# Half swaps strided by two into buffers that are tiles of their own, split input tiles and a new order, in a one-core block of long convolution and MLP

## The chip, the core and the metric

The kernel runs on one core of a Trainium2 chip. The metric is the device time of the program in microseconds (us). The kernel before takes 302.73 us, the median of three runs (301.24, 302.73 and 303.07).

The engines are named as in the profile: PE (TensorE, matmul; PEld its weight loads), DVE (VectorE), ACT (ScalarE), POOL (GpSimd) and SP (SyncE, which here only issues DMAs). L613 is line 613 of the kernel before.

## What is computed

All tensors are bf16, with S = 2048 tokens, D = 640 channels and F = 1728. The reference, cut to what matters:

```python
mod = (silu(c) @ w_mod).reshape(6, D)          # sa, ca, ga, sb, cb, gb
h = layernorm(x) * (1 + ca) + sa               # x is A_q
x = x + ga * A(h, k, v, shift_k, ssm_k, ssm_D)
h = layernorm(x) * (1 + cb) + sb
x = x + gb * B(h, w1, w2, w3, w4)

def A(q, k, v, ...):
    kv = shift_conv(k, 4 taps) * v
    y = irfft(rfft(kv, 4096) * rfft(ssm_k, 4096))[:2048]   # along the tokens, by channel
    return q * (y + kv * ssm_D)

def B(h, ...):
    g = gelu(layernorm(h) @ w1)                # its four quarters are shifted by 1, -1, 2, -2 tokens
    h1 = h + shifted(g) @ w2
    return h1 + gelu(layernorm(h1) @ w3) @ w4
```

## The kernel before

**Order.** The body does not issue instructions directly. It makes tasks (`add`, L90), each with the engines that may run it, and the ranges that it reads and writes. A string `ORDER` (L26 to L66) lists all 1046 tasks by number, each with a letter for its engine (P for PE, D for DVE, A for ACT, G for POOL, S for SP) and, for PE, the PSUM slots (four, 0 to 3) that it takes. `run` (L120) emits the tasks in that order. Each engine works through its own tasks in the order of the list and waits where an operand is not there yet. The order of a DMA queue is thus also an order of the list.

**Memory.** The large buffers are single tiles that are used several times over: Ra (ssm_k, then x), Rb (slots, tables of products, then y), T01 with its halves T0 and T1, R3 (first the spectrum of ssm_k), R5 (k and v, then the spectrum of kv), RG (stage-2 tables), RH, RK and RQ.

**FFT stage.** ssm_k is loaded (L228) and k and v are loaded transposed (L233), in five blocks of 128 channels. L444 folds ssm_D into the first element of ssm_k. `k_shift` makes the shift convolution with diagonal weights on PE (L463) and multiplies by v on DVE (L468). `to_slots` (L394) transposes 32x32 blocks on DVE. The Fourier transform of length 4096 has two steps of matmuls: `stage1` (L407) against F1bd, and `stage2_half` (L427) against tables Gs in RG. The tables hold sines and cosines that are made here: angles (L287 to L294, or L302 to L310 with POOL), Sin on ACT (L316, L321), a negated copy (L348), and copies over the partitions by DMA (L353, L354). In the output of stage 2, the real parts are in partitions 0 to 63 and the imaginary ones in 64 to 127. Results leave PSUM by ACT (L207) or DVE (L209).

**inverse1** multiplies the two spectra, ten blocks of 128x2048. A product of complex numbers needs one factor with its real and imaginary halves exchanged. Two DMAs of 256 KB (L613) make that copy of the block `kx` into one of four buffers KSY (a part of RG, two of RK, one of Rb); the first is issued by SP and the second by POOL. DVE then makes two products (L617), PE multiplies them by EA and EB (L628, L629; made at L370), and ACT or DVE evicts.

```python
for o in range(2):
    dma("SP" if o == 0 else "POOL", 256, lambda q, o=o: q.dma_start(
        ky[64 * o:64 * o + 64, :], kx[64 - 64 * o:128 - 64 * o, :]), ...)
```

**inverse2** (L661) needs all of inverse1 and tables in RH (L576 copies them there by 16 DMAs), takes groups of up to three token tiles and two PSUM slots at a time, and its result y goes to Rb.

**Transition and MLP.** x is loaded by `x_load` (L525), tiles 0 to 7 early, 8 to 11 and 12 to 15 later. Statistics of the first layer norm come by L539 and L540 on DVE, or L547 and L548 on ACT. The modulation vectors are products on PE (L493), evicted at L508. `make_q` (L592, L594, L601, L602) normalizes and modulates a tile, `chain_a` (L737, L740) multiplies by y and adds to x, `square_sum` (L729, ACT) and `ln_finish` (L702 to L717, with a power on POOL at L715) give the statistics, `chain_b` (L755, L756) the second modulation, and `chain_c` (L594 or L724) normalizes and turns the tile over by PE (L772; copied at L778 or L780) or by a DMA transpose (L765). Then `mm_w1` (L818, L828; gelu at L820, L834), `mm_w2` (L873; L880 on DVE), `mm_w3` (L907; gelu at L911) and `mm_w4` (L928, L937; L960 to L966 on DVE), and the output is stored (L969, and L987 for the last tile). w1 and w2 are loaded at L992 to L995 into RG, w3 at L1012 into T0, w4 into T1. The buffers g3 of the second gelu are in R5.

Of the kernel before, what the change touches and what calls it, by code (L numbers as in the profile page):

```python
# [8 lines left out]
BF = mybir.dt.bfloat16  # L9
# [17 lines left out]
0S 2S 19G 18D 50G 20D 21G 23D 22D 25A 4S 3S 1S 6S 27G 29D 36G 37G 28D 5S 8S 9S 11S 68G 10S 69D 24A 26G 88P:0 72G 73D 31A 30A 32D 38G 66D 89A 84P:1 85A  # L27
67D 90P:2 91A 86P:3 87D 39G 40A 102P:0 103A 100P:1 76P:2 70G 104P:0 41D 49G 101A 77A 42G 43G 105A 106P:3 107A 44A 45G 33S 47S 46S 71D 34S 12S 35S 48S
184S 181S 183S 182S 13S 14S 116P:1 92P:2 98P:0 74D 75D 117D 7S 99A 118P:3 119D 114P:0 15S 112P:1 113D 93A 110P:2 16S 115A 111A 96P:3 97A 94P:0 95D
82P:2 83A 80P:1 81A 78P:3 108P:0 51D 109A 52D 54A 56G 57D 53A 122P:2 79D 155P:1 156A 153P:0 154A 151P:3 152A 123D 157P:2 136D 120P:1 121D 173P:0 158A  # L30
55G 174A 171P:3 172A 177P:2 178D 175P:1 176A 161P:0 162D 141P:3 142A 167P:2 168D 147P:1 148A 58G 59G 163P:0 164D 165P:3 166A 137P:2 138A 145P:1 146A
230D 17S 149P:0 150A 190D 188D 126P:3 127D 139P:2 140A 60A 143P:1 199S 144A 124P:0 125D 179P:2 180A 187D 169P:3 170A 234P:1 235A 244P:2 159P:0 160A
128P:3 231D 242P:1 243A 245A 130P:0 61G 62G 186D 63G 64A 238P:1 239A 129D 131D 232D 248P:2 65G 196S 249A 246P:3 247A 185D 189G 191A 252P:0 202S 253A
134P:1 135D 132P:2 133D 236P:3 240P:1 237A 260P:0 261A 233D 250P:2 251A 241D 423D 200P:3 201A 258P:0 259D 319G 208S 192G 268P:2 269A 318S 197P:3 205S
198A 266P:1 267A 272P:2 273D 270P:3 271A 203P:0 284P:1 285A 292P:2 211S 204D 278P:3 279A 417D 276P:0 277A 342S 293D 426D 209P:1 210D 294P:2 295D 226S
290P:3 222G 291A 280P:1 281D 229G 227S 264P:0 274P:2 275D 343G 223G 265A 256P:3 262P:1 420D 206P:0 207D 257A 225G 254P:2 255D 282P:3 263A 286P:0
288P:1 287D 224G 312P:2 220S 283A 289A 212P:3 321D 320D 218G 213D 313A 328D 304P:0 305A 308P:1 316P:2 317A 217S 216G 302P:0 219S 214G 418D 228S 298P:2
215S 324P:3 325D 309A 221G 327G 326S 329D 322P:1 303A 336D 306P:0 299A 421D 323A 310P:2 296P:3 307A 334S 335G 337D 350S 297A 311A 300P:1 330P:0 301A
351G 332P:3 344D 345D 331A 314P:2 333A 315A 359G 340P:1 341A 338P:0 352D 348P:3 349A 353D 346P:2 358S 347A 360D 361D 354P:1 367G 339A 356P:3 368D 366S
369D 355A 364P:2 357A 375G 362P:0 376D 372P:1 374S 377D 401S 193A 363A 382S 370P:3 373A 384D 383G 385D 380P:0 378P:1 365A 392D 390S 391G 393D 422D  # L40
419D 424D 402P:2 427D 194D 403D 371A 388P:3 381A 379A 407S 389A 428D 386P:0 387A 416G 425D 396P:1 397A 394P:3 395A 398S 399P:0 400D 432P:12 429A 430D
434D 433A 489D 502A 510D 195G 413S 490D 491A 511D 530D 408P:3 513D 404S 405P:0 406A 531D 409A 512A 440S 492G 494D 475P:12 476A 477A 515D 532A 462P:03
463A 410S 411P:1 493G 495D 514G 435S 533D 534G 496A 497D 498G 441G 535D 464A 516D 536D 518D 499D 412A 517A 469P:20 537A 471A 519G 500P:3 538D 539G
414P:1 465G 470A 558D 449S 501D 520D 521P:3 436S 415A 507P:0 522A 443S 559D 560A 540D 541P:2 437S 542A 466P:13 431D 561D 562D 563A 564D 508A 546P:2
467D 468A 547A 548P:1 565G 448S 570D 528P:0 571D 566D 572D 567D 549A 573A 446S 568D 505P:3 506A 569A 574G 575G 447S 509G 529A 503D 523D 504D 621D 622D
472P:21 473A 526P:3 527A 623A 579D 580P:0 581A 576D 439S 543A 524D 577P:2 525D 624D 578D 625D 444S 438S 550P:3 627D 480S 551D 481S 626A 590P:0 591A
445S 482S 552A 588P:2 589A 595P:3 459D 628G 633D 629D 634D 553G 630D 631D 632A 635D 637D 636A 479S 554G 555D 556P:0 557A 592P:2 486S 596D 597A 638G
641A 639D 478S 488G 610P:3 612P:0 611A 593D 608P:2 606P:3 544D 594A 598D 613A 599G 474D 460A 603D 600D 601P:1 604P:0 609A 457D 607A 442S 454A 602A
640S 642S 651P:2 649P:3 461G 650A 450D 487S 652A 485S 605D 673P:0 667P:1 451D 545D 668A 674A 452G 582D 583D 484S 689D 690D 456A 458G 584D 585D 656P:3
692D 693D 653P:2 483S 614P:1 654D 655A 657D 694A 615D 659G 658A 671P:0 695D 660G 664D 665P:2 691A 661D 662P:3 663D 453D 669P:1 696G 701A 702D 703D  # L50
666A 735P:3 455G 672A 670A 697D 698D 699D 705G 737P:2 736A 739P:0 733P:1 616D 704A 643D 644D 645D 700A 738A 706G 709A 675P:32 710S 586D 587D 740A 755D
756D 757A 646A 707D 708S 758D 759D 717P:0 714D 761G 760A 762G 734A 763A 767D 777A 768D 711A 769D 719P:1 764D 780D 676P 718A 720A 721P:0 724P:1 647D
712D 765D 766A 677D 678D 770A 680S 771G 772G 683D 741P:32 648D 773D 774S 722D 775A 776S 785P:0 725D 726A 783P:1 713D 723A 824D 617S 825D 742P 821D
822D 827D 679S 681S 826A 743D 682S 727G 728G 731D 732S 823A 784A 828G 829A 786A 787P:3 729D 730S 833D 834D 835D 830D 831D 832A 837D 684D 685S 836A
620S 838G 790P:1 788D 789A 839D 840S 799P:0 791D 805P:3 806A 781D 841D 715D 716D 881D 749D 793G 792A 882D 842S 883A 803P:1 804A 794G 795A 796S 845P:2
846A 797D 778D 779D 884D 843P:3 844A 885D 887D 800A 801P:1 802A 618S 847P:2 848D 782D 941D 850P:3 851D 852A 886A 849A 619S 687S 798S 865P:0 866A
859P:1 860A 863P:2 807P:30 861P:1 744D 750D 753S 942D 944D 745S 853D 854G 855A 888G 893A 943A 752S 857A 889D 864A 945G 890D 856S 808P 858S 809D 891D
946A 947D 948D 950D 894D 862A 892A 895D 896A 897G 925P:2 926A 898G 751S 815D 747S 919P:3 901D 686S 920A 923P:1 899D 921P:0 949A 951G 922A 902S 900S
905P:2 906A 688S 903P:3 904A 952D 953S 956P:0 957A 954P:2 955A 907P:3 908D 910P:0 810D 958G 748S 959P:2 911D 913G 746S 816D 819S 924A 962P:1 867P:30
960D 817S 963D 813S 754S 912A 993P:2 909A 914G 812S 868P 915D 916S 917D 918S 977P:1 978A 994D 995A 996G 997G 971P:2 820S 972A 869D 998A 875D 927P:30  # L60
818S 964A 814S 811S 876D 961A 965D 966G 973P:1 967A 999S 969A 970S 870D 929D 974A 1028P:2 930D 975P:3 928P 968S 1000P:1 1001A 931S 935D 1002P:0 934S
976A 979P:13 981D 1003A 1006P:0 871S 873S 1004P:1 879S 1005A 872S 874S 936D 980P 987D 1029A 937S 933S 1026P:1 939S 1007A 877S 932S 988D 1024P:2 1025A
1032D 880S 878S 982D 983S 1008P:30 986S 991S 1027A 989S 1033D 1010D 938S 940S 1022P:2 1011D 1023A 1014S 1013S 1009P 1016D 984S 985S 1017D 1030P:13
1034D 992S 990S 1015S 1012S 1018S 1019S 1020S 1035D 1037S 1036S 1021S 1038S 1031P 1040D 1039S 1041D 1043A 1045A 1042S 1044S
# [72 lines left out]
def kernel(  # L137
# [20 lines left out]
    Ra = mem.tile([P, 10240], BF, name="Ra")  # L158
# [6 lines left out]
    RK = mem.tile([P, 4096], BF, name="RK")  # L165
# [9 lines left out]
    sT = Ra[:].rearrange("p (b n) -> p b n", b=ND)  # L175
    sL = Rb
    kvL = Rb
    x_all = Ra[:].rearrange("p (a d) -> p a d", d=D)
# [4 lines left out]
    Gs = RG[:, 0:6144].rearrange("p (k n) -> p k n", k=32)  # L183
# [6 lines left out]
    wm = [(R[:, o:o + 1600].rearrange("p (b n) -> p b n", b=ND), (k, o, o + 1600)) for R, k, o in ((RH, "RH", 0), (RH, "RH", 1600), (RK, "RK", 0))]  # L190
    TAB = [[Rb[:, (2 * i + j) * 2048:(2 * i + j + 1) * 2048] for j in range(2)] for i in range(2)]
    KSY = [(RG[:, 6144:8192], ("RG", 6144, 8192)), (RK[:, 0:2048], ("RK", 0, 2048)), (RK[:, 2048:4096], ("RK", 2048, 4096)), (Rb[:, 8192:10240], ("Rb", 8192, 10240))]
# [34 lines left out]
    for b in range(ND):  # L227
        dma("SP", 512, lambda q, b=b: q.dma_start(sT[:, b, :], A_ssm_k[b * P:(b + 1) * P, :]), w=[("Ra", 2048 * b, 2048 * b + 2048)], rate=390.0)  # L228
# [13 lines left out]
    s32 = mem.tile([P, 1], F32, name="s32")  # L242
    s32o = mem.tile([P, 1], F32, name="s32o")
    s64 = mem.tile([P, 1], F32, name="s64")
    s64t = mem.tile([P, 1], F32, name="s64t")
    pci = mem.tile([P, 2], I32, name="pci")
    offi = mem.tile([P, 2], F32, name="offi")
    offc = mem.tile([P, 6], F32, name="offc")

    def f(e):  # L250
        nc.vector.memset(mhalf[:], -0.5)
        nc.vector.memset(b_pos[:], PI_LO)
        nc.vector.memset(b_neg[:], -PI_LO)
        nc.vector.memset(stat[:], 0.0)
# [279 lines left out]
    def ln1_stats(A):  # L534
        st = small.tile([P, 2, 6], F32, name="ln1_st", tag="ln1_st", bufs=4)

        def f(e):
            for i in range(2):
                nc.vector.bn_stats(st[:, i, :], x_all[:, A, i * 320:(i + 1) * 320])  # L539
# [539 lines left out]
```

## Time and profile before

| | |
|---|---|
| median of three runs | 302.73 us |
| span of the profiled execution | 298.7 us |
| median less profiled span | 4.03 us |
| first matmul of the spectrum stage | 8.12 us |
| last of the products of inverse1 begins | 92.6 us |
| first matmul of mm_w3 | 135.74 us |
| last turn before PE works without a gap | 140.31 us |
| last matmul | 293.69 us |
| bytes moved by DMA | 35.76 MB |

The profile is of one execution, whose span is counted from its first to its last recorded event; the time of a run covers more, so a span is set against the span and a time against times. In the page, a group of instructions is a line of the kernel with an engine, an operation, the tiles it writes and reads, and a count. "idle before" is the time that the engine stood still ahead of it, with what ended it. A view of stretches gives the busy time of each engine between two instants. A view of waits gives who waited for whom, in sum.

### The profile page before, as it was taken

Reading aid. Unit: us, or ns where it says so; the run is one execution under the profiler, and the core shown is the slowest. Engines: PE = TensorE matmul, PEld = TensorE weight load, DVE = VectorE, ACT = ScalarE, POOL = GpSimd, SP = SyncE. Lnnn points to the kernel's source line nnn. Section 1 sums busy time; section 2 is a strip of 40 time slices with the busy share of each in tenths; the row PEclk is TensorE's granted clock in tenths of the full one; section 3 lists DMA queues with packets and bytes.
Section 4 is the critical chain, followed back from the end, with each engine's and each line's share of the span. In section 5 each row is a group of like instructions: output and inputs, shape, how many; then the busy total and the mean of one; then the engine's idle time right before and its main releaser. Section 6 shows DMA issues by size and latency. Waiting matters only on the chain.

```text
span 298.7 us, 7890 instructions
## 1 busy us (share of the span) xinstructions
PE 269.7 (90%) x3176; PEld 208.5 (70%) x3182; DVE 218.2 (73%) x438; ACT 208.3 (70%) x341; POOL 104.8 (35%) x237
## 2 busy tenths in 40 slices
PE   0999999999989766869999999999999999999993
PEld 0666755777878436648878677787788767887871
DVE  8998999999999998898759589886361544212442
ACT  4799989999999789979868775766854705431200
POOL 5864364453216591434275426120421321100000
PEclk9999999999999859799999999999999999999999
DMA  6999999898999920563700203223113030510112
GB/s 215 275 215 184 225 137 246 225 217 221 229 253 281 280 65 2 153 203 69 273 4 0 46 5 68 56 46 60 41 40 80 5 89 6 63 43 23 29 52 60
DMA packets 58356, 35.76 MB, mean 120 GB/s; under 512 B 40032, under 2 KB 55008, under 8 KB 58320
## 3 DMA queue, kind: packets, MB, share of 16 engines
q1 hardware_dynamic: 57136, 32.01, 46.3%
q0 software_dynamic: 1088, 3.21, 4.1%
q8 instruction: 25, 0.41, 0.6%
q14 instruction: 11, 0.09, 0.1%
q10 hardware_dynamic: 96, 0.04, 0.1%
HBM read 16.31 MB, written 2.62 MB: 63 GB/s over the span
## 4 chain that ended last, share of the span: by engine, by line
PE 51%; DVE 13%; ACT 11%; DMA 10%; POOL 6%; issue 5%; SPq 2%; DVEq 0%; POOLq 0%; ACTq 0%
PE ps_w L937 17%; PE ps_w L907 14%; ACT T L207 5%; DMA Ra<-in_A_q_dram 5%; PE ps_w L873 4%; PE ps_w L818 3%; PE ps_s L427 3%; ACT RG L729 3%; DVE Rb L617 3%; PE ps_ksh L463 2%; POOL lnv L715 2%; PE ps_s L407 2%; DMA RK<-R 2%; DVE R L756 2%; PE ps_mod L493 2%
## 5 line engine op out<-in xcount | busy, mean ns | idle before, releaser
L907 PE MATMUL ps_w<-R,T 128*128 128x256 bf16 (+1 forms) x630 | 63.8, 261 | 0.7 <-DMA R<-RH 0.7
L907 PEld LDWEIGHTS <-T 128*128 128x128 bf16 x630 | 55.5, 98 | 7.9 <-issue 2.0
L937 PE MATMUL ps_w<-T,R 128*128 128x320 bf16 x416 | 59.1, 299 | 0.0
L911 ACT ACTIVATE R<-ps_w 128x1024 bf16<-128x1024 f32 (+2 forms) x36 | 28.8, 827 | 41.9 <-PE ps_w L907 41.9
L937 PEld LDWEIGHTS <-R 128*128 128x128 bf16 x416 | 40.5, 98 | 15.2
L960 DVE TENSOR_TENSOR T<-ps_w,R 128x640 bf16<-128x640 f32 x15 | 12.3, 822 | 35.4 <-PE ps_w L928 18.1
L207 ACT CAST T<-ps_s 128x1024 bf16<-128x1024 f32 x32 | 30.4, 1029 | 3.2 <-PE ps_s L407 3.1
L207 ACT CAST R<-ps_s 128x960 bf16<-128x960 f32 (+1 forms) x35 | 30.8, 964 | 1.8 <-PE ps_s L427 1.6
L407 PE MATMUL ps_s<-F1bd,Rb 128*128 128x256 bf16 x160 | 23.3, 298 | 8.7 <-DVE Rb L394 8.1
L729 ACT ACTIVATE RG<-R 128x640 bf16<-128x640 bf16 x32 | 23.5, 734 | 9.9 <-DVE R L880 6.7
L407 PEld LDWEIGHTS <-Rb 128*128 128x128 bf16 x160 | 16.7, 107 | 14.7 <-DVE Rb L394 8.6
L873 PE MATMUL ps_w<-RG,R 128*128 128x320 bf16 x160 | 23.2, 299 | 2.1 <-ACT R L820 2.1
L715 POOL TENSOR_TENSOR lnv<-lnv,mhalf 128x2 f32<-128x2 f32 (+1 forms) x29 | 22.5, 775 | 2.3
L427 PE MATMUL ps_s<-T,RG 64*128 64x160 bf16 x512 | 21.2, 230 | 0.8 <-ACT R L207 0.6
L880 DVE SCALAR_TENSOR_TENSOR R<-ps_w,R 128x640 bf16<-128x640 f32 x16 | 12.9, 819 | 11.8 <-PE ps_w L873 11.6
L427 PEld LDWEIGHTS <-RG 64*128 64x128 bf16 x512 | 17.7, 94 | 5.1 <-issue 4.6
L818 PE MATMUL ps_w<-R,RG 128*128 128x256 bf16 (+1 forms) x200 | 20.0, 259 | 1.3 <-DMA R<-RK 0.6
L873 PEld LDWEIGHTS <-R 128*128 128x128 bf16 x160 | 15.4, 98 | 8.2 <-ACT R L820 2.4
L629 PE MATMUL ps_i<-EB,Rb 128*128 128x128 bf16 x160 | 19.0, 219 | 1.5 <-DVE Rb L617 1.4
L818 PEld LDWEIGHTS <-RG 128*128 128x128 bf16 x200 | 17.1, 102 | 3.5 <-issue 2.0
L628 PE MATMUL ps_i<-EA,Rb 128*128 128x128 bf16 x160 | 19.0, 219 | 0.4 <-ACT R L207 0.3
L714 POOL TENSOR_TENSOR lnv<-stat,lnv 128x2 f32<-128x2 f32 x19 | 4.0, 212 | 40.9 <-ACT RG L729 28.7
(178 smaller groups left out, 513.5 us busy)
## 6 DMA issues: line engine op xcount, KB each, us to landing
Ra<-in_A_ssm_k_dram SPq DMA_DIRECT2D x5, 512.0 KB, 5.7
R<-in_w_mod_dram SPq DMA_DIRECT2D x6, 400.0 KB, 6.0
out_dram<-RH SPq DMA_DIRECT2D x60, 40.0 KB, 1.6
T<-in_B_w_dram SPq DMA_DIRECT2D x5, 432.0 KB, 6.2
RH<-in_w_mod_dram SPq DMA_DIRECT2D x4, 400.0 KB, 4.4
Ra<-in_A_q_dram SPq DMA_DIRECT2D x4, 320.0 KB, 6.6
RK<-R SPq DMA_DIRECT2D x5, 256.0 KB, 4.5
RK<-R POOLq DMA_DIRECT2D x5, 256.0 KB, 5.3
```

Source lines behind the costliest of these rows:

```text
L207: nc.scalar.copy(dst, src(ps.tile))
L407: nc.tensor.matmul(psv[:, ml, :], lhsT=xL[:, s0:s0 + P], rhs=F1r, start=True, stop=True)
L427: nc.tensor.matmul(psv[:, g, j], lhsT=Gs[p, k, 64 - 64 * cc:192 - 64 * cc], rhs=T1h[h][p, cc * 32 + k], start=(cc == 0), stop=(cc == 1), t ...
L628: nc.tensor.matmul(psv[:, w, :], lhsT=Av[:, r_, :, g_], rhs=EAf, start=True, stop=False)
L629: nc.tensor.matmul(psv[:, w, :], lhsT=Bv[:, r_, :, g_], rhs=EBf, start=False, stop=True)
L715: nc.gpsimd.tensor_tensor(rs, rs, mhalf[:, 0:n], ALU.pow)
L729: add("ACT", 0.74, lambda e: nc.scalar.activation(junk, src, ACT.Square, scale=float(D) ** -0.5, accum_out=stat[:, li, 1, t:t + 1]), r=[sk ...
L818: nc.tensor.matmul(pt[:, fb, 0:cw], lhsT=w1_sb[:, b, 160 * fb:160 * fb + P], rhs=hT[:, b, 0:cw], start=(b == 0), stop=(b == ND - 1))
L873: nc.tensor.matmul(pt[:, hf, 0:320], lhsT=gsf[:, fb, c0:c0 + P], rhs=w2_sb[:, fb, 320 * hf:320 * hf + 320], start=(fb == 0), stop=(fb == 4))
L907: nc.tensor.matmul(pt[:, fl, 0:cw], lhsT=w3_sb[:, b, fb * P:(fb + 1) * P], rhs=xT[:, b, 0:cw], start=(b == 0), stop=(b == ND - 1))
L911: nc.scalar.activation(g3[g % 2][:, f0:f0 + fn, 0:cw], ps.tile[:, 0:fn, 0:cw], ACT.Gelu_apprx_tanh)
L937: nc.tensor.matmul(bank(i, hf), lhsT=gg[:, fb, i * P:(i + 1) * P], rhs=w4_sb[:, fb, 320 * hf:320 * hf + 320], start=(fb == 0 and i == 0), ...
```

## The change

The following is done, all at once.

- The tables Gs have 256 instead of 192 columns for each of 32 k, so that they fill RG, and their columns are arranged so that the outputs of stage 2 have real and imaginary parts interleaved over the partitions. The negated copy is made by two strided operations where there was one, for each half of the tables. The copies over partitions are 262 KB instead of 196 KB, six of them.
- The half swap exchanges even and odd partitions, so each of its two DMAs reads and writes every second partition. Its second DMA may be issued by SP as well. The four buffers KSY are RaY, RaZ, RK0 and RK1, which are tiles of their own.
- Ra is split into RaX (x tiles 0 to 7), RaY (8 to 11) and RaZ (12 to 15), which hold blocks of ssm_k first; its last block goes to RH. RK is split into RK0 and RK1.
- EA and EB are made by four operations over all partitions, with a sign for each partition, instead of eight over halves; four tiny operations on DVE make that sign and an index.
- x, w1 and w2 have no place after the first inverse2 prescribed to them any longer; a part of x may be issued by POOL. w3 is loaded into R5, and g3 lies in T0.
- inverse2 is one task with one PSUM slot for each half of its output, instead of one with two slots. The matmuls are the same.
- A Gelu of one column is added on ACT, after the last Sin; the gelus of the MLP follow it.
- `ORDER` is new as a whole (1056 tasks). Among its differences: on SP, the transposing load of the third block of k stands behind one of the table copies and the loads of x tiles 0 to 7; all 16 copies into RH are issued by SP; POOL issues 5 DMAs before the first mm_w3 instead of 19; all of inverse2 stands ahead of the first turn.

The diff, cut to its core:

```diff
-    Ra = mem.tile([P, 10240], BF, name="Ra")
+    RaX, RaY, RaZ = (mem.tile([P, n], BF, name=nm) for n, nm in ((5120, "RaX"), (2560, "RaY"), (2560, "RaZ")))
...
-    RK = mem.tile([P, 4096], BF, name="RK")
+    RK0, RK1 = (mem.tile([P, 2048], BF, name=nm) for nm in ("RK0", "RK1"))
...
-    Gs = RG[:, 0:6144].rearrange("p (k n) -> p k n", k=32)
+    Gs = RG[:].rearrange("p (k n) -> p k n", k=32)
+    Gv = RG[:].rearrange("p (k c j t) -> p k c j t", k=32, c=2, t=2)
...
-    KSY = [(RG[:, 6144:8192], ("RG", 6144, 8192)), (RK[:, 0:2048], ("RK", 0, 2048)), (RK[:, 2048:4096], ("RK", 2048, 4096)), (Rb[:, 8192:10240], ("Rb", 8192, 10240))]
+    KSY = [(RaY[:, 0:2048], ("Ra", 5120, 7168)), (RaZ[:, 0:2048], ("Ra", 7680, 9728)), (RK0[:], ("RK", 0, 2048)), (RK1[:], ("RK", 2048, 4096))]
...
-        add(("POOL", "DVE"), {"POOL": 1.48, "DVE": 0.35}, lambda e, k2s=k2s: eng_of[e].tensor_scalar(Gs[:, k2s, 128:192], Gs[:, k2s, 0:64], -1.0, None, ALU.mult),
-            r=[wk[:3]], w=[wk], port=0.4)
+        for i in range(2):
+            add(("POOL", "DVE"), {"POOL": 1.49, "DVE": 0.62}, lambda e, k2s=k2s, i=i: eng_of[e].tensor_scalar(Gv[:, k2s, 0, :, i], Gv[:, k2s, 1, :, 1 - i], 1.0 - 2.0 * i, None, ALU.mult),
+                r=[wk[:3]], w=[wk[:3] + ("g0",)], port=0.4)
...
-        dma(("SP", "POOL"), 196, lambda q, lo=lo: q.dma_start(RG[64:128, lo], RG[0:64, lo]), w=[lk], rate=215.0)
+        dma(("SP", "POOL"), 262, lambda q, lo=lo: q.dma_start(RG[64:128, lo], RG[0:64, lo]), w=[lk], rate=215.0)
...
-                            nc.tensor.matmul(psv[:, g, j], lhsT=Gs[p, k, 64 - 64 * cc:192 - 64 * cc], rhs=T1h[h][p, cc * 32 + k],
+                            nc.tensor.matmul(psv[:, g, j], lhsT=Gs[p, k, 128 * cc:128 * cc + 128], rhs=T1h[h][p, cc * 32 + k],
...
-        ky, kk = KSY[i % 4]
+        ky, kk = KSY[i % 4 if i < 8 else i - 6]
...
-            dma("SP" if o == 0 else "POOL", 256, lambda q, o=o: q.dma_start(ky[64 * o:64 * o + 64, :], kx[64 - 64 * o:128 - 64 * o, :]), r=[kxk], w=[kk + ("y",)], rate=222.0)
+            dma("SP" if o == 0 else ("SP", "POOL"), 256, lambda q, o=o: q.dma_start(ky[o::2, :], kx[1 - o::2, :]), r=[kxk], w=[kk + ("y",)], rate=390.0)
...
-    w3_sb = T0[:, 0:ND * FP].rearrange("p (b n) -> p b n", b=ND)
+    w3_sb = R5[:, 10240:10240 + ND * FP].rearrange("p (b n) -> p b n", b=ND)
...
+    add("ACT", 0.25, lambda e: nc.scalar.activation(s64[:], b_pos[:], ACT.Gelu_apprx_tanh),
+        r=[("consts", 0, 1), ("sin", 0, 1)], w=[("gelu", 0, 1), ("scol", 0, 1)])
...
-    y0 = [("Rb", 0, D)]
...
-    x_load(8, 12, y0)
-    x_load(12, NT, y0)
+    x_load(8, 12)
+    x_load(12, NT)
```

## Prediction

> **What bounds the kernel now.** I read the page first, for which engine is full, then the busy time by stretches cut at the stage borders, because the shares of the whole span mix stages with different limits. In the page, a digit is tenths of one of 40 slices of 7.47 us.
>
> ```profile
> PE 269.7 (90%) x3176; PEld 208.5 (70%) x3182; DVE 218.2 (73%) x438; ACT 208.3 (70%) x341; POOL 104.8 (35%) x237
> PE   0999999999989766869999999999999999999993
> ...
> DVE  8998999999999998898759589886361544212442
> ACT  4799989999999789979868775766854705431200
> ```
>
> The columns of the stretches are: stretch, its length, PE, PEld, DVE, ACT, POOL busy, TensorE clock, DMA share, GB/s.
>
> ```profile
> 10.00:27.00 17.00, 16.54 (x131) 11.41 (x131) 16.48 (x19) 16.23 (x21) 9.15 (x10) 1.00 1.08 204
> 27.00:53.60 26.60, 26.07 (x318) 16.78 (x318) 25.04 (x32) 24.62 (x32) 14.57 (x23) 1.00 1.10 212
> 53.60:93.80 40.20, 37.63 (x621) 31.99 (x619) 39.72 (x42) 39.28 (x48) 13.52 (x27) 1.00 0.92 226
> 93.80:140.30 46.50, 35.16 (x798) 26.71 (x798) 41.98 (x111) 41.32 (x87) 23.69 (x61) 0.85 0.52 145
> 140.30:294.00 153.70, 152.43 (x1308) 120.27 (x1308) 85.28 (x205) 82.86 (x152) 37.30 (x104) 1.00 0.23 53
> ```
>
> Three stages follow. In the FFT stage (10 to 93.8) DVE is idle for 0.52+1.56+0.48=2.56 us and ACT for 0.77+1.98+0.92=3.67, so the work of these two sets its length. PE shows as busy there too (37.63 of 40.20), but the ends of matmuls are modelled, and the two evicting engines, busier still, are what frees its PSUM. In the transition (93.8 to 140.3) DVE is idle for 4.5 and ACT for 5.2 us. From 140.3 PE is full (152.43 of 153.70). So only what comes before 140.3 can move the end, and there only DVE and ACT work, or waits of these two.
>
> Next, the operation that the change names. The half swap (L613) feeds the second product of each inverse1 (L617):
>
> ```profile
> L617 DVE TENSOR_TENSOR Rb<-R,R x10: 1212/1215/1221, 69.6 to 91.4; 128x2048 bf16<-128x2048 bf16 x10
> L617 DVE TENSOR_TENSOR Rb<-R,RK x5: 1209/1216/1225, 73.8 to 92.6; 128x2048 bf16<-128x2048 bf16 x5
> its engine sat idle before it (us, times) until:
> who waited for it (us, times):
> ...
> DMA to landing us min/median/max: 3.1/5.2/7.3
> ```
>
> The list of what DVE waited for is empty, and the last line (from the view of L613) says that a swap lands after 5.2 us. It is wholly hidden. The waits of the whole span, by queue and engine, hold two more that the change touches:
>
> ```profile
> SPq L1012 <- PE ps_i L661: 16.0, 1, 16.0
> POOL lnv L714 <- ACT RG L729: 28.7, 15, 5.6
> ```
>
> The first is w3's load, which may not start before the last inverse2 has read T0. It lands before the first mm_w3 at 135.74, and DVE and ACT are loaded meanwhile: it costs nothing now. Last, DVE where the convolution of k and v ends and the loads of them matter:
>
> ```profile
> 50.04 0.83 DVE L539 BATCH_NORM_STATS2 ln_st<-Ra 128x6 f32<-128x320 bf16 x2
> 50.91 0.21 DVE L540 BATCH_NORM_AGGREGATE mv<-ln_st 128x2 f32<-128x12 f32 x1
> 51.03 2.52 DVE L468 TENSOR_TENSOR R<-ps_ksh,R 128x1024 bf16<-128x1024 f32 x2
> ```
>
> The last v transpose is issued at 45.68 to 48.05 and lands some 5.0 later (median of L233), at about 50.7; L468 takes it at 51.03. There is almost no slack here.
>
> **The Trainium skill.** "SBUF — State Buffer", section "Door 1: The DMA port swizzle", says that partitions 0 to 63 reach 8 of 16 ports and measured 196 GB/s, against 328 for all 128. A stride of two over partitions touches all ports by that table. The trace agrees as far as it goes: 230 GB/s at a DMA share of 0.94 in 60 to 90, where the swaps run, and 333 GB/s at 1.00 in 125 to 130, where w3 is loaded. "ScalarE: Activation LUTs", section "What ACT_TABLE_LOAD costs", gives about 1283 ns for the load and 1380 ns for a drain. The trace has 1.283 us before L834 at 115.56 and the gelu at 116.85, so no further drain; the trace decides. "DMA: Bandwidth & Descriptors", section "Issuing engines are not separate DMA queues", says that another issuing engine saves only the sequencer's time; no run here isolates that.
>
> **The change part by part.** Counts are differences of the two hand-written orders, durations are rows of the profile.
>
> 1. *Strided swap, own tiles, ring of four.* DMA time falls; an estimate by the two rates of that SBUF page is 1.3 to 0.8 us for 256 KB. Gain 0, since L617 waits for no DMA. What hides it is the other products ahead on DVE (20 of 1.22 us in 68 to 94); were that cover gone, or the two halves made to wait for each other, the first swap's landing would show, so the loss is 0 to 5.2 us, taken 0.
> 2. *Tables.* The upper and lower copies grow from 6x196 to 6x262 KB: 0.39 MB, at 204 GB/s 1.9 us of DMA before v's last part. The negation of L348 (0.743 on DVE, 1.52 on POOL) becomes four, one on DVE and three on POOL: POOL +3.0, which makes the second half's copies about 1.5 us later (the chain of sines ended near 19.3). The four small DVE operations are 4x0.15=0.6. The strided forms are not in the trace; I take the same durations, ends -0.1 and +0.9 in all.
> 3. *DVE and ACT to the end of inverse1.* DVE: stage-1 evictions 2x1.215 fewer, stage-2 evictions 3x1.15 more, one row of LN statistics (1.1) fewer, angles +0.56, step 2's +0.6, make_q -0.49, norm +0.44, modulation -0.48, L444 -0.17: together about +0.4. ACT: 2x1.03-3x0.99+1.95 (statistics)+2x0.43: about +1.95, against 3.67 idle. Packed in the new order with these durations from a first matmul at 8.2 (before 8.12), DVE ends the last product at 93.0 instead of 93.79: **-0.8**. With the +0.4, that recovers 1.2 of DVE's 2.56 idle (ends -2.2 and +0.4).
> 4. *k and v later.* On SP's queue the transpose of k's third block (21.11 before) now stands behind a table copy and the x loads (about 27.5), each of those issuing in about 0.5 and landing after 7.8. Everything that SP issues afterwards is k and v, for k_shift on PE and L468 on DVE, and then transposes, stage 1 and 2. Cost: v4 lands between 50.7 (the same bytes reordered) and 57.1 (all 6.4 us carried through); by bytes alone 52.6. DVE packed wants it at 51.0. Ends 0 and +6.1; I take **+0.5**, a third of the 1.6 by which 52.6 passes 51.0, since DVE was not packed there before (1.56 idle).
> 5. *x, w1, w2 early; w3 into R5.* Before, these were issued at 92.82 to 94.4 behind the ring part in RG; now x 8 to 15 can go after products 4 and 5. Work of LN statistics moves with them (counted in 3 and 6); waits removed that cost 0 to 3, taken inside 6.
> 6. *Transition.* DVE: make_q -1.23, statistics -2.22, inverse1 evictions +1.21, inverse2 evictions +1.15, ln_finish -1.2, norm -0.40, turns +0.9: -1.8. ACT +0.3. Halving inverse2 changes none of its 512 matmuls. The table load (1.28) moves from the middle of the first mm_w1 to behind the last inverse1 eviction, where ACT has as much to do; 0, with +0.25 for the dummy gelu in ACT's sum. Followed by hand along the new order, the first normed tile is later (113.3 for 109.25, since all inverse2 evictions stand ahead), but mm_w2 of tile 1 is at 126.7 for 128.03, and the turn that starts the full stretch at 138.3 to 138.7 for 140.31: **-1.5** (ends -4.5, all of DVE's idle, and +1.5).
> 7. *From there on.* PE has the same tasks left, 153.4 us, and 5 us of tail. Its waits are 2.5 us in all: 0 (ends -1 and +1).
>
> Sum: -0.8+0.5-1.5=-1.8. The profiled span is 298.7, so 296.9; the median of the runs, 302.73, is 4.03 above the profiled span, which gives 300.9.
>
> **The rivals.** *A, the sum above*: 300.9, own range 298.5 to 303.3. For: stage work is nearly equal. Chance 0.46.
> *B, the idle time is recovered.* The shares of the stretches speak for it: 2.6 us of DVE in the FFT stage and 4.5 in the transition, and the x loads at 94.37 to 108.14 are in the chain that ended last. With 2.3 of the one and 3.9 of the other gone: 302.73-6.2=296.5. Against: in-order engines with POOL's small powers (12.5 us of waits for L729 in the transition) between them. Chance 0.20.
> *C, slower: k and v late.* One mechanism, in step 4. If the whole delay of 6.4 us of the k transpose comes through, v4 lands at 57.1, 6.1 after DVE wants it; without step 4's 0.5 the sum is -2.3, so +3.8: 306.5. It decides from a landing at 53.3, where the gain is gone (51.0+2.3); over 1% slower is from 56.3. For: DMA share 1.10 in 27 to 53.6, so no spare rate. Against: 0.39 MB is only 1.9 us. Chance 0.20.
> *D, the change does nothing.* The swap was hidden and the loads' waits too; the order's differences cancel: 302.7, 302 to 303.5. For: L617 waits for nothing. Chance 0.14.
>
> **How the numbers follow.** The likeliest is A, 300.9. About 1%, 3.0 us, is what a measurement of this kernel can tell from no change. Below 299.7: a third of A (0.15), nearly all of B (0.20), a little of D: 0.37. Above 305.76: two thirds of C (0.14) and a little of A through a false wait (0.02): 0.16. Between: 0.47. The range 296.0 to 306.0 leaves out some of B (0.08) and over half of C (0.11).
>
> **What would show it.** Right: no DMA ahead of L617 in the new trace, smaller landing times; last product near 93 to 94; the last k_shift product at 51 to 52; the last turn before the full stretch near 138.5, and some 153 us of PE after it. Step 4 fails if DVE idles before k_shift; step 6 if DVE and ACT idle less than 2 us or over 5 in the transition; step 1 if L617 waits for a swap. The whole would be wrong if PE's full stretch is itself shorter or longer than 153.4.

## The result and the profile after

The change makes the kernel slower by a little. Over 20 runs each, its median is 303.88 us against 301.65 us, and the ratio of the two is 1.0069, with a 95% interval of 1.0047 to 1.0091. The forecast was 300.9 us against 302.73, which is a ratio of 0.994.

The page of the changed kernel is of an execution that took 306.04 us, second slowest of its 20, with a span of 304.2. A run thus lasts 1.84 us longer than its span. With that, the page of the kernel before is of an execution of about 300.5 us (an estimate: 298.7+1.84), at the fast end of its 20, and the 4.03 us that the prediction put between span and median were mostly luck of the draw. The two pages differ by 5.5 us, the medians by 2.2. A second page of the changed kernel (e1, below, span 302.8) stands between and shows the same places.

Line numbers are those of each kernel: in the changed one, L639 are the products (L617 before), L635 the swap (L613), L491 the k_shift product (L468), L450 stage 2 (L427), L430 stage 1 (L407), L370 the last table copies (L354), L598 the copies into RH (L576), L561 the statistics on DVE (L539). First the lines of its page that answer to those of the kernel before:

```profile
PE 270.5 (89%) x3182; PEld 210.5 (69%) x3182; DVE 215.7 (71%) x435; ACT 215.4 (71%) x356; POOL 98.1 (32%) x226
PE   0799899998876965788999989999999999999993
...
DVE  8999988999898799888889997994150413401422
ACT  4699898999988599899999978997585220152020
```

DVE shows 8 and 7 in its 13th and 14th digits (about 91 to 106 us), where the kernel before had nines. To see how much, I cut both executions at the same events, not at the same times: the start of the last pair of k_shift products, of the first product of inverse1, the end of the last product, the last turn, and the last matmul. Columns as before (stretch, length, PE, PEld, DVE, ACT, POOL, clock, DMA share, GB/s). The kernel before:

```profile
8.00:51.03 43.03, 41.98 (x434) 27.87 (x440) 41.08 (x49) 39.12 (x48) 23.49 (x28) 1.00 1.09 207
51.03:68.44 17.41, 17.04 (x227) 12.84 (x226) 16.93 (x20) 16.52 (x23) 9.43 (x21) 1.00 0.91 228
68.44:93.79 25.35, 23.12 (x413) 20.82 (x410) 25.22 (x25) 25.29 (x31) 6.23 (x10) 1.00 0.95 236
93.79:140.30 46.51, 35.16 (x798) 26.71 (x798) 41.99 (x111) 41.33 (x87) 23.70 (x61) 0.85 0.52 145
140.30:293.70 153.40, 152.14 (x1308) 120.19 (x1308) 85.28 (x205) 82.86 (x152) 37.30 (x104) 1.00 0.23 53
```

And the changed kernel:

```profile
8.00:54.97 46.97, 43.59 (x451) 28.29 (x452) 44.00 (x51) 42.30 (x55) 26.62 (x38) 1.00 1.10 210
54.97:72.61 17.64, 17.45 (x258) 13.25 (x258) 17.13 (x24) 16.37 (x20) 2.16 (x6) 1.00 0.67 202
72.61:101.04 28.43, 22.88 (x365) 20.12 (x360) 25.02 (x26) 24.82 (x31) 5.18 (x9) 0.95 0.82 262
101.04:145.80 44.76, 34.12 (x811) 28.81 (x810) 39.66 (x100) 40.15 (x83) 22.56 (x64) 0.80 0.50 148
145.80:299.20 153.40, 152.29 (x1311) 120.07 (x1308) 82.19 (x206) 88.44 (x165) 36.79 (x99) 1.00 0.21 43
```

The lengths differ by +3.94, +0.23, +3.08, -1.75 and 0.00 us. So the full stretch of PE is unchanged, the transition is 1.75 us shorter, and the FFT stage is 7.25 us longer. Of the 7.25, DVE's work is 2.92 (86.15 busy against 83.23) and its idle time 4.33 (6.89 against 2.56).

Most of the new idle time lies in the stretch of the products (3.41 us for 0.13 before), and there it has a name. This is the answer for the products, where the list of waits was empty before:

```profile
L639 DVE TENSOR_TENSOR Rb<-R,RK x6: 1218/1225/1227, 79.0 to 99.8; 128x2048 bf16<-128x2048 bf16 x6
L639 DVE TENSOR_TENSOR Rb<-R,RaY x2: 1221/1224/1226, 72.6 to 85.1; 128x2048 bf16<-128x2048 bf16 x2
...
its engine sat idle before it (us, times) until:
  DMA RK<-R: 3.0, 4
  DMA RaZ<-R: 0.3, 1
```

Five of the products wait for their swap, 3.3 us in all, four of them for the buffers RK. In the view of L635 a swap lands, that is, its data has arrived, 5.1 us after its issue (2.4 to 6.9), hardly sooner than before (5.2). SP's own list of instructions says why the buffers RK are late:

```profile
64.86 11.53 SPq L598 DMA_DIRECT2D RH<-RK  x16
76.49 0.54 SPq L635 DMA_DIRECT2D RK<-R  x1
...
90.21 1.10 SPq L635 DMA_DIRECT2D RK<-R  x2
```

The 16 copies into RH, which read RK1, occupy SP for 11.53 us, from the first issue to the end of the last. The halves of the swaps into RK0 and RK1 that SP issues for blocks 2 and 3 (of 0 to 9) stand behind the last of them. In the kernel before SP issued 7, POOL 9, and SP was free at 68.7. The swap of block 8 starts only at 90.21, when the product that reads block 6's copy ends (88.96+1.22), because the ring (the buffers that the swaps use in turn) is two deep for the last two blocks: they go to the buffers of blocks 6 and 7, not of 4 and 5.

### The profile page after: what moved, and what is told of

Its sections match the earlier page's. It is cut to its first block, busy times and chain, and to the rows that moved or that the text cites. A ratio compares the mean times of both kernels' runs of the same rounds, so it can differ in the third digit from the quotient of the medians.

```text
span 304.2 us, 7915 instructions
## 1 busy us (share of the span) xinstructions
PE 270.5 (89%) x3182; PEld 210.5 (69%) x3182; DVE 215.7 (71%) x435; ACT 215.4 (71%) x356; POOL 98.1 (32%) x226
## 4 chain that ended last, share of the span: by engine, by line
PE 50%; DVE 13%; DMA 6%; ACT 3%; issue 2%; SPq 1%; ACTq 0%; DVEq 0%
PE ps_w L931 17%; PE ps_w L961 16%; PE ps_w L897 7%; PE ps_w L842 5%; DMA R<-in_w_mod_dram 2%; DMA RK<-R 2%; DVE R L778 2%; DVE Rb L639 2%; DMA R<-RK 1%; PE ps_w1x L852 1%; SPq L635 1%; DVE Rb L219 1%; DVE RaX L762 1%; PE ps_w L952 1%; DVE R L777 1%
## 5 line engine op out<-in xcount | busy, mean ns | idle before, releaser
L935 ACT ACTIVATE T<-ps_w 128x1024 bf16<-128x1024 f32 (+2 forms) x36 | 29.4, 831 | 50.3 <-PE ps_w L931 44.5
L931 PE MATMUL ps_w<-R,R 128*128 128x256 bf16 (+1 forms) x630 | 63.9, 261 | 0.0
L931 PEld LDWEIGHTS <-R 128*128 128x128 bf16 x630 | 55.5, 98 | 6.4 <-issue 0.3
L961 PE MATMUL ps_w<-T 128*128 128x320 bf16 x416 | 59.2, 299 | 0.0
L961 PEld LDWEIGHTS <-T 128*128 128x128 bf16 x416 | 40.2, 98 | 16.4 <-issue 1.3
L217 ACT CAST T<-ps_s 128x1024 bf16<-128x1024 f32 x34 | 32.6, 1035 | 4.6 <-PE ps_s L430 4.6
L430 PE MATMUL ps_s<-F1bd,Rb 128*128 128x256 bf16 x160 | 22.6, 289 | 9.5 <-DVE Rb L417 9.1
L217 ACT CAST R<-ps_s 128x960 bf16<-128x960 f32 (+1 forms) x32 | 29.0, 983 | 1.9 <-PE ps_s L450 1.9
L430 PEld LDWEIGHTS <-Rb 128*128 128x128 bf16 x160 | 16.3, 103 | 15.7 <-DVE Rb L417 9.4
L450 PE MATMUL ps_s<-T,RG 64*128 64x160 bf16 x512 | 21.6, 230 | 1.7 <-DMA RG<-RG 0.9
L737 POOL TENSOR_TENSOR lnv<-lnv,mhalf 128x2 f32<-128x2 f32 (+1 forms) x29 | 21.6, 746 | 2.3
L450 PEld LDWEIGHTS <-RG 64*128 64x128 bf16 x512 | 17.6, 94 | 6.2 <-issue 4.2
L217 ACT CAST T<-ps_i 128x1024 bf16<-128x1024 f32 x19 | 18.8, 1053 | 3.7 <-PE ps_i L651 3.6
L897 PEld LDWEIGHTS <-R 128*128 128x128 bf16 x160 | 15.5, 98 | 7.7 <-ACT R L844 1.8
L486 PE MATMUL ps_ksh<-R,RQ 128*128 128x512 bf16 x80 | 19.0, 380 | 0.6 <-DMA R<-in_A_k_dram 0.5
```

The costliest lines, as they stand in the source:

```text
L217: nc.scalar.copy(dst, src(ps.tile))
L430: nc.tensor.matmul(psv[:, ml, :], lhsT=xL[:, s0:s0 + P], rhs=F1r, start=True, stop=True)
L450: nc.tensor.matmul(psv[:, g, j], lhsT=Gs[p, k, 128 * cc:128 * cc + 128], rhs=T1h[h][p, cc * 32 + k], start=(cc == 0), stop=(cc == 1), tile ...
L737: nc.gpsimd.tensor_tensor(rs, rs, mhalf[:, 0:n], ALU.pow)
L897: nc.tensor.matmul(pt[:, hf, 0:320], lhsT=gsf[:, fb, c0:c0 + P], rhs=w2_sb[:, fb, 320 * hf:320 * hf + 320], start=(fb == 0), stop=(fb == 4))
L931: nc.tensor.matmul(pt[:, fl, 0:cw], lhsT=w3_sb[:, b, fb * P:(fb + 1) * P], rhs=xT[:, b, 0:cw], start=(b == 0), stop=(b == ND - 1))
```

## The experiments

Each ran in five rounds beside the kernel before, in four groups (e1 to e4, e5 to e8, e9 to e12, e13 to e15), each on another chip. The numbers are ratios to the kernel before on the same chip, with 95% intervals; one below 1 is faster. The changed kernel itself ran only in the first group (1.0085) and for the result (1.0069), so the later groups are set against these two across chips. T1 is the theory of the new waits for swaps, T2 that of the new order (DVE's work and k and v), T2a that of later tables, T3 that the new tables and strides cost by themselves.

**e1, the changed kernel again.**

> The changed kernel, unchanged, for a second profile: the profiled execution of it was the second slowest of its 20 runs (306.04 us, median 303.88) and that of the kernel before one of its fastest, so the two pages overstate the difference. All theories: ratio 1.004 to 1.009. T1 (waits for half swaps): DVE idle for 2 to 3.5 us ahead of L639 on its DMAs again. T2 (the new order puts more work of DVE ahead of the last k_shift, and k and v come later): the last L491 again begins at 53.5 to 55 us instead of 51.0. Chance alone (rival): both shrink below 1 us and only the sum of DMA noise is left.

Measured: 1.0085 (1.0056 to 1.0113). L639 waits 3.0 us for swaps again, and the last pair of L491 begins at 56.0 us. So neither is an accident of one page. Its view of PE's waits from 8 to 60 us shows a further one that the kernel before did not have:

```profile
PE ps_s L450 <- DMA RG<-RG: 1.1, 1, 1.1
...
PE ps_ksh L486 <- DMA R<-in_A_k_dram: 0.2, 1, 0.2
```

Stage 2 waits for the last table copy, whose landing takes 7.3 us here and 4.8 before; k is hardly waited for. The two last copies are not issued later than before. These are SP's own instructions, of the kernel before and of the changed one:

```profile
24.45 1.91 SPq L354 DMA_DIRECT2D RG<-RG  x2
```

```profile
22.47 1.91 SPq L548 DMA_DIRECT2D RaX<-in_A_q_dram  x2
24.48 1.88 SPq L370 DMA_DIRECT2D RG<-RG  x2
```

What is new is that two loads of x are issued ahead of them, and that they are larger.

**e2, the new buffers and tables in the order of before.**

```diff
-ORDER of the change
+ORDER of the kernel before, renumbered; the ten added tasks beside their like
```

> The changed buffers, tables and strided swaps, with the instructions of each engine in the order of the kernel before (added tasks beside their like). T2 (order): the last L491 goes back to about 51 us, ratio 0.995 to 1.001. T1 (swaps): the ring is as shallow as in the changed kernel for the last two blocks, so 1 to 2 us of waits ahead of L639 stay, ratio 1.001 to 1.005. T3 (larger tables, strided copies and negations cost time by themselves): ratio 1.007 or more.

Measured: 1.0569 (1.0520 to 1.0617), on T3's side, but eight times the loss of the change itself. L639 waits 5.5 us for swaps, the first four table copies occupy SP for 7.6 us (2.7 before), the last v transpose is issued at 52.65 instead of 45.68, and the statistics wait 1.9 us for x. So the new buffers and tables in the old order are far slower than in the new one, and going back to the old order does not take the loss away. It does not tell more, because where I put the ten tasks is a choice, and some of the delay may come from it.

**e3, halves instead of the stride.**

```diff
-q.dma_start(ky[o::2, :], kx[1 - o::2, :])
+q.dma_start(ky[64 * o:64 * o + 64, :], kx[64 - 64 * o:128 - 64 * o, :])
```

(with the tables and EA, EB arranged to match)

> The changed kernel, with real and imaginary parts in halves of the partitions again, so the swap exchanges partitions 0 to 63 with 64 to 127; rings, tables' size and order as changed. If the stride makes the swap faster and L639 now waits for swaps (T1), they land later here: waits ahead of L639 grow by 1 to 3 us, ratio 1.010 to 1.017. If the stride is worth nothing (T2, rival), the ratio stays at 1.004 to 1.009 and the landing times at about 5.3 us. If the stride costs (T3), the ratio falls below 1.004.

Measured: 1.0275 (1.0237 to 1.0313). Beside e1 on the same chip, the stride is worth 1.0275/1.0085, or 1.9%, in this order. The swaps land after 6.3 us, where e1 has 4.3, and DVE's products wait for them longer (the view of L639):

```profile
its engine sat idle before it (us, times) until:
  DMA RK<-R: 5.8, 3
  ACT T L217: 1.1, 1
```

These waits for swaps grow by 2.8 us (5.8 for 3.0), about half of what the medians differ by (311.15 and 305.31). The swap's speed matters now, because the swap is no longer hidden.

**e4, the ring of four to the end.**

```diff
-        ky, kk = KSY[i % 4 if i < 8 else i - 6]
+        ky, kk = KSY[i % 4]
```

(and the loads of x 8 to 15 behind the blocks that use their place)

> The changed kernel, but the copies of the last two blocks go to the first two buffers of the ring, so each waits for the block four before it, not two; x tiles 8 to 15 are loaded after these blocks. T1: the waits of 0.76 and 0.96 us ahead of the last two L639 go, 1 to 2 us saved, ratio 1.000 to 1.004, unless x becomes late for its statistics. T2: no change, ratio 1.004 to 1.009.

Measured: 1.0055 (1.0033 to 1.0077). Only one wait for a swap is left, of 1.4 us near 83 us. The direction is T1's, but the intervals of e4 and e1 overlap, so this run alone shows no gain.

**e5, copies split.** Six of the 16 copies into RH are issued by POOL.

```diff
-228S 232S 219S 223S 229S 222S
+228G 232G 219G 223G 229G 222G
```

> The changed kernel, with 6 of its 16 copies into RH issued by POOL instead of all by SP. T1a (the wait ahead of the product of the fourth block comes from SP: 16 copies at 0.72 us each keep it from 64.9 to 76.4, and the swap into RK1 must wait for the last of them): SP is done by about 72, the waits of L639 near 79 to 84 us (1.3 us) go, 0.5 to 1.3 us saved, ratio 1.004 to 1.007 where the changed kernel has 1.0085 beside the same chip. Rival (that wait is set by landing under DMA load, not by SP): waits stay, ratio 1.006 to 1.010.

Measured: 1.0042 (1.0019 to 1.0066), waits of 2.1 us for RK and 0.4 for RaZ instead of 3.0. T1, with the same reservation on its size.

**e6, negations on DVE.** The two of the second half of the tables move from POOL to DVE, right behind its four small operations.

```diff
-46G 52D
+52D 46D 47D
...
-34S 47G 81P:0
+34S 81P:0
```

> The changed kernel, with the two negations of the second half of the tables on DVE (about 0.45 us each) right after its sines, instead of on POOL (1.6 each). T2a (later tables hold up the FFT stage: PE waits 1.1 us for a table copy at 32 us): copies 2.3 us earlier, the waits for RG go, the last L491 1 to 2 us earlier, ratio 1.003 to 1.006. Rival (DVE's own load decides): 0.9 more work on DVE ahead, ratio 1.008 to 1.012.

Measured: 1.0047 (1.0027 to 1.0067). The ratio lies in T2a's range, the wait for RG is gone from the view, and the last L491 begins at 55.5, where e1 had 57.3 and the page after 56.3. But the copies are not 2.3 us earlier: SP issues the last two at 24.78 (24.88 in e1), behind two loads of x, and they land after 6.8 us. In e13, with the same move, they land after 7.6 us and the wait is back. So the POOL negation is not shown to be what makes the tables late, and the interval overlaps that of e1.

**e7, the stride alone in the kernel before.**

```diff
-q.dma_start(ky[64 * o:64 * o + 64, :], kx[64 - 64 * o:128 - 64 * o, :])
+q.dma_start(ky[o::2, :], kx[o::2, :])
```

> The kernel before, with its swap read and written at every second partition[...]; the exchange itself is left out (even go to even, odd to odd), so the result is not the reference's. If the swap was wholly hidden before (my step 1, T1): ratio 0.998 to 1.002. If its traffic slowed other transfers that count (w_mod, w1, x): 0.990 to 0.997.

Measured: 1.0229 (1.0179 to 1.0280). Both expectations missed. The swaps land after 3.1 us, sooner than in any other kernel here, and yet the products wait. These are SP's waits, and then those of DVE:

```profile
SPq L613 <- PE ps_i L629: 10.2, 1, 10.2
```

```profile
DVE Rb L617 <- PE ps_i L628: 2.7, 2, 2.4
DVE Rb L617 <- DMA Rb<-R: 2.2, 1, 2.2
```

The swap into Rb waits 10.2 us for matmuls. These read the products, which lie in other columns of Rb than the swap writes. In the kernel before, no swap of SP waits for L628 or L629; most of their waiting is for DVE's products (9.4 us, five times).

**e8, ring of four and copies split together.**

> The changed kernel with the ring of four to the end and 6 copies on POOL. T1: nearly all of the 3.0 to 3.4 us of waits ahead of L639 go, ratio 0.998 to 1.003. T2 (work ahead of the last k_shift): 1.004 to 1.008, since the 4 us there stay.

Measured: 1.0009 (0.9987 to 1.0031), which is clear of e1 and of the result. The change's loss is gone, with the table copies as late as they were (landing 7.7 us). The page, of an execution 2 us above this run's median, still has 2.1 us of waits for swaps; the page of e13, which holds both edits too, has 0.5.

**e9 and e10, tables and k ahead of x.** On SP, k's third block and the last table copies go ahead of the x loads; e10 has this with e4, e5 and e6.

```diff
-49S 187S 186S 36S 50S 184S 185S 7S 12S
+49S 12S 36S 50S 187S 186S 184S 185S 7S
```

(SP's words alone)

> The changed kernel, but SP issues k's third block and the last two table copies ahead of the x loads, as in the kernel before; nothing else differs. T2a (later tables: these copies land after 7.3 us in the changed kernel, 4.8 before, and PE waits 1.1 us for them at 32 us): landing back to about 5, no wait for RG, the last L491 1 to 2 us earlier, ratio 1.002 to 1.006 where the changed kernel has 1.007 to 1.0085. Rival (the larger tables' traffic and the work of DVE ahead decide): 1.006 to 1.010.

> The changed kernel with the ring of four, 6 copies on POOL, the negations on DVE and the tables first. T1 and T2a together: both new waits gone, what is left of the change is its shorter transition, ratio 0.990 to 0.998, faster than both kernels. Rival (work of DVE ahead of the last k_shift is what remains, 3 us of it): 0.998 to 1.003.

Measured: 1.0141 (1.0113 to 1.0169) and 1.0130 (1.0096 to 1.0164). Both missed. The copies land after 3.7 us in e9, but the statistics stand earlier in the new order of DVE than their x now comes:

```profile
DVE ln_st L561 <- DMA RaX<-in_A_q_dram: 3.6, 1, 3.6
```

In e10 that wait is 4.3 us. These two price an order in which x is late (e10 without it is e13, at 0.9982), and decide nothing on T2a; in e9 stage 2 still waits 1.1 us for a table copy, now an earlier one.

**e11 and e12, tiles of their own in the kernel before.** The ring is moved to parts of the input and of RK that are tiles of their own. e11 has the stride (without the exchange), e12 the halves.

```diff
-    KSY = [(RG[:, 6144:8192], ("RG", 6144, 8192)), (RK[:, 0:2048], ("RK", 0, 2048)), (RK[:, 2048:4096], ("RK", 2048, 4096)), (Rb[:, 8192:10240], ("Rb", 8192, 10240))]
+    KSY = [(RaY[:, 0:2048], ("Ra", 5120, 7168)), (RK0[:], ("RK", 0, 2048)), (RK1[:], ("RK", 2048, 4096)), (RaZ[:, 0:2048], ("Ra", 7680, 9728))]
```

> The kernel before with the ring of the swaps in four tiles of their own (x split over three tiles, RK over two, the last block of the other input in RH) and the swap at every second partition, with the exchange itself left out; tables, queues and order as before. T4 (a strided range of partitions is taken for the whole tile, so in e7 the swaps into Rb waited for matmuls that read other columns of Rb): the waits go, ratio 0.997 to 1.003. Rival (the stride slows something else, such as the reads of R3): 1.015 to 1.025, as in e7.

> As e11, but the swap by halves of the partitions as before, exchange included: the split tiles alone. All theories: 0.998 to 1.003; if higher, the placement of the input in RH and the split tiles cost by themselves. The difference to e11 is what the stride is worth with the order of the kernel before: T1 says nothing (within 0.2%).

Measured: 1.0003 (0.9981 to 1.0024) and 1.0007 (0.9981 to 1.0033). In own tiles the loss of e7 is gone, and the stride brings nothing in this order, though swaps land after 4.0 us instead of 5.2. So the swap was hidden before, and the stride needs buffers that share no tile with other data.

**e13, e4, e5 and e6 together.**

> The changed kernel with the ring of four, 6 copies into RH on POOL and the two negations on DVE, SP's order around the x loads as changed. The waits for swaps and for tables gone together (T1 and T2a): e8 gave 1.0009 and the negation 0.002 to 0.004, so 0.996 to 0.999. Rival (the three overlap, the work ahead of the last k_shift then decides): 1.000 to 1.004.

Measured: 0.9982 (0.9961 to 1.0003). The changed kernel's whole loss is taken back, and perhaps a little more. One wait for a swap is left, of 0.5 us, and the stretch of the products has its old length (stretches as above, the products and the transition):

```profile
73.20:98.50 25.30, 22.77 (x385) 20.39 (x379) 24.68 (x26) 24.68 (x32) 3.74 (x8) 1.00 0.89 284
98.50:142.30 43.80, 34.41 (x794) 28.09 (x793) 39.80 (x101) 40.19 (x84) 25.61 (x68) 0.81 0.54 156
```

25.30 us for 28.43 in the changed kernel and 25.35 before; and a transition of 43.80 for 46.51 before. What stays is the start: the products begin at 73.20 instead of 68.44. Tables are still waited for in this page, by 1.3 us, so the gain over e1 is that of e8's two edits, and none is shown for the negations.

**e14, SP's order alone in the kernel before.** Two x loads, two table copies, two x loads, then c and k's third block.

```diff
-34S 12S 35S 48S 184S 181S 183S 182S 13S 14S 7S
+34S 184S 181S 35S 48S 183S 182S 7S 12S 13S 14S
```

> The kernel before, with only SP's order of the change: two x loads, the last two table copies, two x loads, the small load of c, and then k's third block. T2 (k, v and the tables later hold up the FFT stage): the last L468 1 to 4 us later, ratio 1.003 to 1.012. Rival (the order of loads is covered): 0.998 to 1.002.

Measured: 1.0005 (0.9978 to 1.0031). In its page k is late by 1.4 us at k_shift, and the last L468 begins at 53.9 instead of 52.3, as T2 said, but the time is unchanged. In the order of before, this delay costs nothing.

**e15, no early gelu.** An Identity takes its place.

```diff
-nc.scalar.activation(s64[:], b_pos[:], ACT.Gelu_apprx_tanh)
+nc.scalar.activation(s64[:], b_pos[:], ACT.Identity)
```

> The changed kernel with an Identity in place of the Gelu of one column, so the table is loaded ahead of the first real gelu. My step 6 took its move for 0: ratio as changed, 1.006 to 1.009. If the early load pays (1.28 us out of the transition's chain): 1.009 to 1.013.

Measured: 1.0071 (1.0049 to 1.0093), as with it. The table load of 1.28 us is now at 123.58, inside the transition, where e1 has it at 104.53, and nothing is gained or lost that can be measured.

## Why the prediction was wrong

**Step 1 failed**, and it was the larger part. It took the waits for swaps as 0, from an empty list in the kernel before, and named the cover itself: other products ahead on DVE, and 0 to 5.2 us if it were gone. It said nothing on when a swap may start. That time depends on the ring and on the queue. The step calls the ring one of four, but it is two deep at the end, and 16 copies stand ahead of it on SP; both were in front of me in the diff and the order. In the traces the waits are 3.0 to 3.3 us, the sign that the prediction itself named for a failure of this step; undoing both (e8) takes the ratio from 1.0085 to 1.0009. The stride, which I priced at nothing, saves 1.9% in this order, where swaps are waited for, and nothing where they are not (e11, e12).

**Step 3 failed too**, in both of its terms. It took DVE's work as +0.4 us and 1.2 us of its idle time as recovered. From 8.00 us to the end of the last product, the work grew by 2.92 and the idle time by 4.33, of which 3.28 are in the stretch of the products, where step 1's waits are. The 93.0 us came from packing operations by hand and were set against a measured 93.79. DVE's busy time alone would end at 8.0+86.15=94.15, and with the idle time of before at 96.7. So without any new wait the end of the products was due 2.9 us later, not 0.8 earlier. The largest parts of the work are these: five modulations of make_q fall before the end of the last product instead of two (1.4 us); an operation of the tables came from POOL (L325, 0.7); the four small operations took 0.7; and one angle operation of 64 columns took 1.15 us where its like took 0.25. Another 0.9 are transposes that stood ahead of 8.00 before: DVE makes angles first, so the first matmul of the spectrum starts at 8.95 us and not at the 8.2 from which the step packed. No run undoes this; e13 has it too (8.96).

**Step 4, k and v,** was right in the bytes: the last v transpose is issued 1.92 us later (47.60 for 45.68), the estimate was 1.9. But its +0.5 for a wait is not seen: L491 waits for PE only, 1.6 us in all (0.7 before); PE waits 0.5 us for k, and nobody waits for v. In the order of before, e14 finds no cost in the reordered loads. What was late instead is step 2's table copy (0.9 to 1.1 us of waits on PE). The step had a delay of 1.5 us on POOL and gave it no price; but POOL's part is not the cause, since the last copies are issued when they were before, and land later. Rival C had the sign right and the mechanism wrong.

**Step 6, the transition,** was right in its direction: -1.75 us for -1.5. That it comes so close is luck of the page: the same cut gives 43.12 us in e1 and 43.80 in e13, which is -3.4 and -2.7. Counted from the end of the last product, mm_w2 of tile 1 (its eviction by DVE) is at 33.6 us (33.7 forecast, 34.2 before) and the last turn at 44.8 (45.3 to 45.7 forecast, 46.5 before); the first normed tile is later, as was said. The table load is worth nothing that can be measured, as was said (e15). **Step 7** was right to the tenth: 153.40 in both. **Step 5** stays untested by itself; x early is part of the shorter transition, but no run takes it alone.

So the gain came where it was expected, in the transition, and was given back earlier, in waits and work that the change itself puts into the FFT stage. What remains open is the 2.9 us of DVE's work ahead and the late tables: I take them for the reason that e13 is not faster still (its first stretch, 8.00 to 55.60, has 44.20 us of DVE's work and 3.40 of idle time, for 41.08 and 1.95 before), but no run moves that work back, and none has the tables earlier without a late x.

## What to carry to other kernels

A transfer that nobody waits for is hidden by when it starts, so after a change of rings or queues, ask for each buffer which instruction frees it and what stands ahead on the issuing queue, and not only how long the transfer takes. Never set a time that was packed by hand against a measured one: pack both, or add the idle time of the same stretch. Here a faster transfer was worth nothing in one order and two per cent in another.

## What was not expected of the hardware and the program

- A DMA over every second partition lands sooner than one over 64 adjacent partitions: 4.0 us against 5.2 (e11, e12, same bytes and order, but e11 leaves out the exchange), and 4.3 against 6.3 with the exchange in both (e1, e3). That agrees with the Trainium skill, "SBUF — State Buffer", section "Door 1: The DMA port swizzle": the rate depends on how many ports the partitions of a transfer reach, and by its table 64 adjacent ones reach half of them. The two rates that the prediction set beside that page (230 and 333 GB/s) are of different transfers and do not test it.
- The same stride makes the program wait more where the buffer shares a tile with other data: 1.0229 in e7, 1.0003 in own tiles. That the range is taken for the whole tile is my reading of these waits (10.2 us for matmuls of other columns); the profile shows the wait, not its reason.
- Sixteen small DMAs on one queue hold it for 11.53 us. One issue takes 0.59 us in the median, and a copy lands after 2.8. The Trainium skill, "DMA: Bandwidth & Descriptors", section "Issuing engines are not separate DMA queues", says that issuing from several engines saves only the time on the sequencer, usually small beside the DMA itself; here a part of what e8 recovers is such time.
- The strided negation of 512 columns took 0.45 to 0.85 us on DVE (four in the page after and in e6); the only contiguous one, in the kernel before, took 0.74. No cost of the stride shows there.
